# Attention and a gated feed-forward block on one core: DMA transposes replaced by TensorE transposes

## The chip, the cores and the metric

The kernel runs on one NeuronCore of a Trainium2 chip. The metric is the device time of one execution, in microseconds (us); lower is better. Before the change the median of three runs is 333.79 us.

## What is computed

Block-causal attention over 8 batches of 8 heads (576 positions, 64 columns a head) feeds a feed-forward block with a beta-swish. Inputs and the output are float32; inside, the matmuls take bf16 and fp16.

```python
# q, k, v: (8, 8, 576, 64)
scores = q @ k.T / sqrt(64)
mask   = (i // 64) >= (j // 64)              # a block sees itself and the blocks before it
attn   = softmax(where(mask, scores, -1e9))
x      = (attn @ v).transpose(0, 2, 1, 3).reshape(8 * 576, 512)
h      = x @ w_in                            # (4608, 2048)
out    = (h * sigmoid(beta * h)) @ w_out     # (4608, 512)
```

## The kernel before

The program is a list of operations that a planner in the file (class `Plan`, lines 49 to 347) orders before anything is emitted. Each operation has an engine, an assumed duration, dependencies, the buffers that it holds, and a priority. The planner simulates the five queues, the DMA rings and the eight PSUM banks with its own costs, and fixes one order for each engine; the engines then run their queues in order and wait on semaphores. A change of one operation therefore can move others.

The work has two halves that are woven together:

- **Attention**, in units `u = 4 * b + c`: batch b, pair of heads c. Q and K are loaded in float32 (line 749; lines 711 and 676 for the first two batches), cast to bf16 by GpSimd into `QKn` (lines 763, 767; 718), and turned so that the head's columns lie on the partitions, into `QKT`. In batches 0 and 1 TensorE turns them (line 727) and VectorE copies them out of PSUM (line 735). In the other six batches (`QB = 2`) one DMA transpose for two pairs of heads does it, on SyncE's queue (line 774): 22 blocks of 128 columns. Then come QK (line 818, and repeats by the helper at line 446; two heads at a time in half the array each), exp on ScalarE (line 839), attention times V with V's sums in a 65th column (line 882), and the reciprocal and the normalization on VectorE into `xq` (lines 894, 901).
- `xq` is turned too, into the ring `xT`, which holds 5 chunks of 512 rows. In batches 0 to 2 TensorE does it in 5 transposes a unit (line 930), and VectorE or ScalarE copies the 576 columns out (lines 940, 938), in two pieces or, at the end of the ring, three. From batch 3 on (`XB = 3`) a DMA transpose writes it from `xq` (line 918); it writes 640 columns, the last 64 of which the next batch overwrites.
- **Feed-forward**, in 9 chunks of 512 rows: 16 times the first matmul into one bank (line 1119), tanh on ScalarE (1129), and the gate on VectorE (1133) into `gT`; then the second matmul (line 1155 in chunk 0; in the others a form with seven products of half size, line 1040, with sums on VectorE at lines 984 and 1004 and results at 1061, 1064 and 1055), and the store.

The order around the change is set by priorities. Attention of batch b has the priority 994 + 100 * (b - 1.5) + 4.9 * c, chunk r of the feed-forward 1000 + 100 * r + j, so that attention runs about one and a half chunks ahead, and TensorE takes feed-forward matmuls while attention waits. Of the eight PSUM banks, pairs of banks (class "PP") serve QK and the products with V; single banks (class "P1") are banks 4 to 7 as long as pairs are still to come, and serve the first matmul, the second, and the turned pieces. Idle times of TensorE up to 50 us in the plan are filled by matmuls without use (line 534). SyncE's queue holds, in order, the loads of Q, K and V (lines 711, 749, 560, 563), the DMA transposes, and the last stores; ScalarE's queue issues the other stores (line 1071).

Of the kernel before, what the change touches and what calls it, by code (L numbers as in the profile page):

```python
# [16 lines left out]
RC = 512  # L17
# [342 lines left out]
def bass_blockwise_causal_attn__then__act_swish_beta_kernel(  # L360
# [10 lines left out]
    with es:  # L371
# [1 line left out]
            return es.enter_context(nc.sbuf_tensor(name, shape, dt))  # L373

        NQ = 2
        QB, XB, CAST = 2, 3, "POOL"
        NE = 3
        PARTS = [((0, 4, "SP", (4, 5, 0, 1, 2, 3)), (4, 8, "SP", range(2)), (4, 8, "POOL", (4, 5, 2, 3)))] + [((0, 8, "SP", range(6)),)] * 7
        GROUPS = [((0,), (1,), (2,), (3,))] + [((0, 1), (2, 3))] * 7
# [57 lines left out]
        def dve_t(n):  # L437
            return (n + 125) / 0.96
# [164 lines left out]
            return z  # L603


        def blocks(b):
            x0 = S * b % RX
            n = min(5, (RX - x0) // 128)
            return [z for z in ((0, n, x0), (n, 5 - n, 0)) if z[1]]

        xt = []
        early6 = []
        TC = "POOL"
# [2 lines left out]
        for u in range(NU):  # L616
# [126 lines left out]
            elif p == 0:  # L743

                for w, (nm, src) in enumerate((("Q", q), ("K", k))):
                    ts = P.tile("S4")

                    def fl(g, e, ts=ts, src=src, b=b, c=c, n=2 - w):
                        return [g.dma_start(STh[ts.slot].rearrange("p (i t) d -> p i (t d)", t=n),
                                            src[b, 2 * c:2 * c + 4].rearrange("h t d -> (h t d)").rearrange(  # L750
                                                "(i p x) -> p i x", p=128, x=64 * n))]

                    o = P.op("SP", QKI, fl, deps=[o for t in early6 for o in t.users] if b == QB else [],
                             tiles=[ts], xfer=(QX, QKX)[w], prio=u, dma=["d_S4", 0, 1])
                    o.two = w < 1
                    for i in range(2):
                        ld[nm, u + i] = o
                    for a in range(2):
                        def fn(g, e, ts=ts, tn=tn, a=a, w=w):
                            if w:  # L760
                                x = STh[ts.slot][:, 9 * a:9 * a + 5, :]
                                x = bass.AP(x.tensor, x.offset, [x.ap[0], [64, 5], [256, 2], [1, 64]])
                                return g.tensor_copy(QKn[tn.slot][:, a, 768:1408].rearrange("p (t h d) -> p t h d", t=5, h=2), x)  # L763
                            for i in range(2):
                                x = STh[ts.slot][:, 8 * a + i, :]
                                x = bass.AP(x.tensor, x.offset, [x.ap[0], [128, 3], [256, 2], [1, 64]])
                                z = g.tensor_copy(QKn[tn.slot][:, a, 384 * i:384 * i + 384].rearrange(  # L767
                                    "p (t h d) -> p t h d", t=3, h=2), x)
                            return z

                        casts.append(P.op(CAST, 740 if w else 1000, fn, deps=[o], tiles=[ts, tn], prio=u))

                def ft(g, e, tn=tn, td=tt_):
                    return [g.dma_start_transpose(QKT[td.slot][:].rearrange("c a (t n) -> c (a t) n", n=128),
                                                  QKn[tn.slot][:].rearrange("p a n -> p (a n)"))]

                turned = [P.op("SP", 3500, ft, deps=casts, tiles=[tt_, tn], xfer=3762, prio=-1, dma=["d_T", 0, 1])]
            tqk, cps = tt_, turned
            more = [tail] if b < QB else []
            ex = []  # L780
# [132 lines left out]
                m = P.op("DVE", dve_t(640), fm, deps=[av, r], tiles=[pv, ti, tx], prio=-6 if b < 1 else 0)  # L913
                m.same = [r]
            nrm = [m]
            if b >= XB:
                def fy(g, e, tx=tx, c=c, b=b):
                    return [g.dma_start_transpose(
                        xT[:, c, x0:x0 + 128 * n].rearrange("c (t n) -> c t n", n=128),
                        xq[xq_(tx)][:, t0:t0 + n, :].rearrange("p t n -> p (t n)")) for t0, n, x0 in blocks(b)]  # L920

                n = len(blocks(b))
                xt.append(P.op("SP", 1000 * n, fy, deps=nrm + (xt[u - 4:u - 3] if b > XB else []), tiles=[tx], xfer=855,
                               prio=-1, dma=[f"d_TX{n}_", 0, n]))
                continue
            px = P.tile("P1")

            def fx(g, e, tx=tx, px=px):
# [6 lines left out]
            def fy(g, e, px=px, c=c, b=b):  # L935
# [3 lines left out]
                    else:  # L939
                        z = g.tensor_copy(xT[:, c, x0:x0 + n], PSb[:, px.slot, t0:t0 + n])  # L940
                return z
            xt.append(P.op("ACT" if u in (2, 3) else "DVE", 600 if u in (2, 3) else 520, fy, deps=[xp], tiles=[px], prio=-6 if u < 4 else 0))

        for o in P.ops:
            if o.idx > 40 and o.engs == ("PE",) and not o.fill and any(d.engs == ("SP",) or d.engs == ("POOL",) for d in o.deps) and not o.rest:
# [162 lines left out]
        for r in range(NRC):  # L1108
            row = RC * r
            b0, b1 = row // S, (row + RC - 1) // S  # L1110
            xd = [xt[4 * b + c] for b in range(b0, b1 + 1) for c in range(4)]
            tg = P.tile("gT")
            gs, hs = [], []
            for j in range(NJ):
                ph, tt = P.tile("P1"), P.tile("th")

                def fh(g, e, ph=ph, j=j, row=row):
                    for c in range(4):
                        z = g.matmul(PS[:, ph.slot, :], w_in[:, c, 128 * j:128 * j + 128], xT[:, c, row % RX:row % RX + RC],  # L1119
                                     start=(c == 0), stop=(c == 3))  # L1120
                    return z

                o = P.op("PE", 4 * mm(512), fh, deps=xd + [win[j // 4]], tiles=[ph, tg], lat=4 * mm(512) + 170,
                         mode="full", prio=1000 + 100 * r + j)

                hs.append(o)

                def fs(g, e, ph=ph, tt=tt, j=j):
                    return g.activation(th[tt.slot][:], PS[:, ph.slot, :], ACT.Tanh, scale=beta[:, j:j + 1])  # L1129
                a = P.op("ACT", act_t(512, 1), fs, deps=[o, bC], tiles=[ph, tt], lat=act_t(512, 1) + 93, prio=0)  # L1130

                def fg(g, e, ph=ph, tt=tt, tg=tg, j=j):
                    return g.scalar_tensor_tensor(out=gT[tg.slot][:, j, :], in0=th[tt.slot][:], scalar=1.0,  # L1133
                                                  in1=PS[:, ph.slot, :], op0=ALU.add, op1=ALU.mult)
                gs.append(P.op("DVE", dve_t(512), fg, deps=[a] + (spare.users + spare_x.users if r == 1 else []), tiles=[ph, tt, tg], prio=0))

            for b in range(B):
                if any((S * b + a) // RC - RX // RC == r for a in (0, S - 1 if b < XB else 639)):
                    for c in range(4):
                        xt[4 * b + c].deps += hs  # L1140

            if r in FAST:
                fast(r, row, tg, gs)
                continue

            for w, d0, d1 in [(w, 0, DM) for w in range(4)]:
                po, to = P.tile("P1"), P.tile("ost")


                parts = [(4 * a, 4 * a + 4) for a in range(4)]  # L1150
                o = None
                for j0, j1 in parts:
                    def fo(g, e, po=po, tg=tg, w=w, j0=j0, j1=j1, d0=d0, d1=d1):
                        for j in range(j0, j1):
                            z = g.matmul(PS[:, po.slot, 0:d1 - d0], gT[tg.slot][:, j, 128 * w:128 * w + 128],  # L1155
                                         w_out[:, j, d0:d1], start=(j == 0), stop=(j == NJ - 1))
                        return z

                    n = (j1 - j0) * mm(d1 - d0)
                    was = o  # L1160
                    o = P.op("PE", n, fo, deps=gs[j0:j1] + wout[j0 // 4:(j1 + 3) // 4],
                             tiles=[po, tg], lat=n + 170, mode="full",
                             prio=1000 + 100 * r + (16 + w + 0.01 * j0 if w == 0 else
                                                     103 + 5.33 * (w - 1) + 1.33 * j0 / 4))
                    o.after = was
                    plain.append(o)

                def fv2(g, e, po=po, to=to, n=d1 - d0):
                    if e == "ACT":
                        return g.activation(ost[to.slot][:, 0:n], PS[:, po.slot, 0:n], ACT.Copy, scale=0.5)  # L1170
                    return g.tensor_scalar(out=ost[to.slot][:, 0:n], in0=PS[:, po.slot, 0:n], scalar1=0.5,
                                           scalar2=None, op0=ALU.mult)
                x = P.op("ACT", act_t(d1 - d0) + 80, fv2, deps=[o], tiles=[po, to], lat=act_t(d1 - d0) + 160, prio=0)

                def fd(g, e, to=to, row=row, w=w, d0=d0, d1=d1):
                    return [g.dma_start(out[row + 128 * w:row + 128 * w + 128, d0:d1], ost[to.slot][:, 0:d1 - d0])]
                P.op("ACT", 500, fd, deps=[x], tiles=[to], xfer=900, dma=["d_ost", to], prio=-1)
# [71 lines left out]
```

## Time and profile before

| | |
|---|---|
| three runs | 329.07, 333.79, 334.52 us |
| the profiled execution | 332.46 us, of which the span is 330.6 us |
| matmuls, TensorE's clock | 3062 records, 1.00 of full |
| DMA transposes | 12 from QKn to QKT, 24 from xq to xT |
| from issue to landing, median | 7.2 us and 2.7 us |
| DMA moved | 54.20 MB |
| SyncE's queue, share of 16 DMA engines | 61.9% |

A row of busy times gives the time in which an engine ran at least one instruction. Matmuls overlap: one lasts longer than the gap to the next. A row of the groups has the line, the engine, the operation, what is written from what, the number of instructions, the busy time and the mean of one in ns. A row of waits has who waited for whom, the total in us, how many times, and the longest. A chain of waits goes back from the last instruction to whatever released each step; a step on the chain isn't always time that the engine lost, as it may have had other work meanwhile. "PE" is TensorE, "PEld" its weight loads, "DVE" VectorE, "ACT" ScalarE, "POOL" GpSimd, "SPq" SyncE's queue.

### The profile page before, as it was taken

What the parts mean: (1) busy time and instruction counts of PE and PEld (TensorE: products, weight loads), DVE (VectorE), ACT (ScalarE), POOL (GpSimd) and SP (SyncE); (2) the same over time, 40 slices, a digit from 0 to 9 for tenths busy, and PEclk for the clock granted to TensorE, in tenths of its full rate; (3) what the DMA queues carried; (4) which work ended last, traced back from release to release, by engine and by line L of the source; (5) the groups of instructions that cost most, each with busy time, mean ns of one, the idle gap of its engine ahead of it and who ended that gap; (6) DMA issues with size and microseconds to landing.
All of it is one profiled execution on the core that took longest, in us unless ns stands there. A gap on an engine that the chain in (4) does not pass through costs nothing.

```text
span 330.6 us, 7365 instructions
## 1 busy us (share of the span) xinstructions
PE 317.3 (96%) x3062; PEld 197.5 (60%) x2979; DVE 220.3 (67%) x454; ACT 211.8 (64%) x316; POOL 91.5 (28%) x155
## 2 busy tenths in 40 slices
PE   7898999999999999999989999899999999999996
PEld 1363464435677557845655577655566766666685
DVE  5765883777754897367967684289576866666742
ACT  3857964396737976687678855676978445554521
POOL 5962290084183066003910650080000000000000
PEclk9999999999999999999999999999999999999999
DMA  7999999999899999959899999895030310111023
GB/s 221 251 227 238 205 241 197 204 260 234 187 300 215 207 229 217 234 112 217 173 180 184 235 264 205 202 209 110 0 73 2 103 34 32 33 64 35 3 92 129
DMA packets 147442, 54.20 MB, mean 164 GB/s; under 512 B 116672, under 2 KB 146896, under 8 KB 147408
## 3 DMA queue, kind: packets, MB, share of 16 engines
q1 hardware_dynamic: 132560, 40.72, 61.9%
q0 software_dynamic: 5568, 4.36, 8.4%
q10 hardware_dynamic: 9280, 8.65, 7.9%
q8 instruction: 24, 0.39, 0.5%
q14 instruction: 10, 0.08, 0.1%
HBM read 36.71 MB, written 9.44 MB: 140 GB/s over the span
## 4 chain that ended last, share of the span: by engine, by line
PE 64%; DMA 11%; SPq 8%; DVE 6%; POOL 4%; ACT 3%; issue 2%; POOLq 0%; ACTq 0%
PE PS L1119 25%; PE PS L1040 25%; SPq L560 5%; PE PS L818 5%; DMA ST<-in_q_dram 5%; PE PS L882 5%; DMA w_out<-in_moe_w_out_dram 4%; DVE gT L1133 2%; PE PS L1155 2%; ACT E L839 2%; POOL QKn L767 1%; DMA xT<-xq 1%; DVE xq L901 1%; DMA OV<-in_v_dram 1%; POOL Vn L587 1%
## 5 line engine op out<-in xcount | busy, mean ns | idle before, releaser
L1119 PE MATMUL PS<-xT,w_in 128*128 128x512 bf16 x540 | 129.9, 379 | 3.9 <-POOL QKn L763 1.1
L1129 ACT ACTIVATE th<-PS,beta 128x512 f32<-128x512 f32 x144 | 96.6, 701 | 54.4 <-PE PS L1119 49.8
L1133 DVE SCALAR_TENSOR_TENSOR gT<-th,PS 128x512 f16<-128x512 f32 x144 | 95.5, 681 | 34.9 <-ACT th L1129 34.1
L839 ACT ACTIVATE E<-PS 128x1024 bf16<-128x1024 f32 x93 | 92.1, 1031 | 14.6 <-PE PS L818 12.0
L1119 PEld LDWEIGHTS PS<-xT,w_in 128*128 128x128 bf16 x576 | 53.3, 98 | 56.9 <-DVE gT L1133 2.0
L1040 PE MATMUL PS<-w_out,gT 128*128 128x256 f16 x512 | 62.7, 273 | 0.0
L1040 PEld LDWEIGHTS PS<-w_out,gT 128*128 128x128 f16 x512 | 49.3, 98 | 11.0 <-issue 0.4
L587 POOL CAST Vn<-Vs 128x640 bf16<-128x640 f32 (+1 forms) x28 | 20.6, 734 | 101.8 <-DMA Vs<-in_v_dram 100.5
L1061 ACT ACTIVATE ost<-PS 128x512 f32<-128x512 f32 x32 | 19.2, 600 | 30.3 <-PE PS L1040 30.3
L882 PEld LDWEIGHTS PS<-Vn,E 128*128 128x128 bf16 x930 | 31.3, 97 | 5.7 <-DVE E L845 1.8
L882 PE MATMUL PS<-Vn,E 128*128 128x65 bf16 x930 | 32.5, 193 | 1.5 <-DMA xT<-xq 1.5
L818 PE MATMUL PS<-QKT 64*64 64x64 bf16 (+4 forms) x328 | 33.9, 295 | 0.0
L1040 PE MATMUL PS<-OV 128*128 128x256 f16 x256 | 32.3, 273 | 0.0
L767 POOL CAST QKn<-ST 128x384 bf16<-128x384 f32 x48 | 27.2, 594 | 5.5 <-DMA ST<-in_q_dram 2.8
L818 PEld LDWEIGHTS PS<-QKT 64*128 64x128 bf16 (+1 forms) x328 | 13.2, 96 | 25.4 <-issue 10.4
L1040 PEld LDWEIGHTS PS<-OV 128*128 128x128 f16 x256 | 24.0, 98 | 6.9 <-issue 1.9
L901 DVE TENSOR_TENSOR xq<-PS,inv 128x640 bf16<-128x640 f32 x31 | 25.3, 820 | 0.5
L1004 DVE TENSOR_TENSOR OV<-gT 128x1024 f16<-128x1024 f16 x32 | 22.6, 711 | 1.0 <-PE PS L1040 0.4
L845 DVE MEMSET E<- 64x64 uint32 x62 | 6.9, 112 | 22.0 <-ACT E L839 20.0
L1064 DVE SCALAR_TENSOR_TENSOR ost<-PS,ost 128x512 f32<-128x512 f32 x22 | 15.2, 689 | 9.0 <-PE PS L1040 4.5
L763 POOL CAST QKn<-ST 128x640 bf16<-128x640 f32 x24 | 18.8, 784 | 4.9 <-DMA ST<-in_k_dram 3.3
L1155 PE MATMUL PS<-w_out,gT 128*128 128x512 f16 x64 | 16.0, 380 | 0.5 <-DMA w_out<-in_moe_w_out_dram 0.5
(77 smaller groups left out, 185.0 us busy)
## 6 DMA issues: line engine op xcount, KB each, us to landing
out_dram<-ost ACTq DMA_DIRECT2D x32, 256.0 KB, 3.7
ST<-in_q_dram SPq DMA_DIRECT2D x12, 576.0 KB, 6.2
ST<-in_k_dram SPq DMA_DIRECT2D x12, 576.0 KB, 7.2
Vs<-in_v_dram SPq DMA_DIRECT2D x24, 256.0 KB, 4.3
ST<-in_q_dram SPq DMA_DIRECT2D x8, 256.0 KB, 6.2
ST<-in_k_dram SPq DMA_DIRECT2D x8, 256.0 KB, 6.5
w_in<-in_moe_w_in_dram POOLq DMA_DIRECT2D x4, 512.0 KB, 11.3
w_out<-in_moe_w_out_dram POOLq DMA_DIRECT2D x4, 512.0 KB, 10.6
```

Of the source, the lines that this page charges most:

```text
L587: return g.tensor_copy(Vn[t.slot][:, 0:n, g0:g1, 0:64], Vs[ts.slot][:, 0:n, g0:g1, :])
L767: z = g.tensor_copy(QKn[tn.slot][:, a, 384 * i:384 * i + 384].rearrange("p (t h d) -> p t h d", t=3, h=2), x)
L818: z = g.matmul(o, QKT[tqk.slot][r, uu % 2, 768 + 128 * t + y:768 + 128 * t + m + y], x)
L839: return g.activation(y, x, ACT.Exp, scale=0.125)
L882: z = g.matmul(o, eblk(te, t, i, h), Vn[Tv.slot][:, t, 2 * c + h, 0:65], start=(t == 0), stop=(t == i))
L901: return g.tensor_tensor(xq[xq_(tx)][:].rearrange("p i (h d) -> p h i d", h=2), both(pv, 0, 64), x, ALU.mult)
L1004: return P.op("DVE", dve_t(SZ * HC / 2), mk(lambda g: g.tensor_tensor(fo(), fx(), fy(), op)), deps=deps, tiles=tiles, prio=prio)
L1040: x = g.matmul(PS[:, pw.slot, HM * w:HM * w + HM], fa()[:, j, 128 * w:128 * w + 128], fb()[:, j, :], start=first and (pair or w == 0) and ...
L1119: z = g.matmul(PS[:, ph.slot, :], w_in[:, c, 128 * j:128 * j + 128], xT[:, c, row % RX:row % RX + RC], start=(c == 0), stop=(c == 3))
L1129: return g.activation(th[tt.slot][:], PS[:, ph.slot, :], ACT.Tanh, scale=beta[:, j:j + 1])
L1133: return g.scalar_tensor_tensor(out=gT[tg.slot][:, j, :], in0=th[tt.slot][:], scalar=1.0, in1=PS[:, ph.slot, :], op0=ALU.add, op1=ALU.mult)
L1155: z = g.matmul(PS[:, po.slot, 0:d1 - d0], gT[tg.slot][:, j, 128 * w:128 * w + 128], w_out[:, j, d0:d1], start=(j == 0), stop=(j == NJ - 1))
```

## The change

The two kinds of DMA transposes are taken out. For batches 2 to 7, each two pairs of heads of Q and K are turned by TensorE in 22 transposes, which go to three PSUM banks (8, 8 and 6 blocks); the first and the third are copied to `QKT` by VectorE, the second by ScalarE. The three bank operations depend on the same casts as the DMA transpose did, and have TensorE's priority of that unit. For batches 3 to 7, `xq` is turned as in the batches before: 5 transposes a unit into one bank, copied to `xT` in pieces. These copies go to ScalarE for units 2 and 3 as before, and now also for odd units from 5 on, otherwise to VectorE; the planner's assumed time for such a copy on VectorE is 700 instead of 520 ns from batch 2 on. The ring's rule for rows that are still in use loses its exception for the 640 columns.

```diff
-        QB, XB, CAST = 2, 3, "POOL"
+        QB, CAST = 2, "POOL"
+        TURN = ((0, 8, "DVE"), (8, 16, "ACT"), (16, 22, "DVE"))
...
-                def ft(g, e, tn=tn, td=tt_):
-                    return [g.dma_start_transpose(QKT[td.slot][:].rearrange("c a (t n) -> c (a t) n", n=128),
-                                                  QKn[tn.slot][:].rearrange("p a n -> p (a n)"))]
-
-                turned = [P.op("SP", 3500, ft, deps=casts, tiles=[tt_, tn], xfer=3762, prio=-1, dma=["d_T", 0, 1])]
+                turned = []
+                for n0, n1, eng in TURN:
+                    pt = P.tile("P1")
+
+                    def ft(g, e, tn=tn, pt=pt, n0=n0, n1=n1):
+                        x = QKn[tn.slot][:].rearrange("p a n -> p (a n)")
+                        for i in range(n0, n1):
+                            z = g.transpose(PSb[:, pt.slot, 128 * (i - n0):128 * (i - n0) + 128],
+                                            x[:, 128 * i:128 * i + 128], identB[:])
+                        return z
+
+                    n = n1 - n0
+                    o = P.op("PE", n * 56, ft, deps=casts, tiles=[tn, pt, tt_], lat=n * 56 + 170, mode="full", prio=pr(u))
+
+                    def fc(g, e, td=tt_, pt=pt, n0=n0, n1=n1):
+                        y = QKT[td.slot][:].rearrange("c a n -> c (a n)")[:, 128 * n0:128 * n1]
+                        x = PSb[:, pt.slot, 0:128 * (n1 - n0)]
+                        return g.activation(y, x, ACT.Copy) if e == "ACT" else g.tensor_copy(y, x)
+
+                    turned.append(P.op(eng, act_t(128 * n) if eng == "ACT" else dve_t(128 * n), fc, deps=[o],
+                                       tiles=[pt, tt_], prio=0))
...
-            if b >= XB:
-                def fy(g, e, tx=tx, c=c, b=b):
-                    return [g.dma_start_transpose(
-                        xT[:, c, x0:x0 + 128 * n].rearrange("c (t n) -> c t n", n=128),
-                        xq[xq_(tx)][:, t0:t0 + n, :].rearrange("p t n -> p (t n)")) for t0, n, x0 in blocks(b)]
-
-                n = len(blocks(b))
-                xt.append(P.op("SP", 1000 * n, fy, deps=nrm + (xt[u - 4:u - 3] if b > XB else []), tiles=[tx], xfer=855,
-                               prio=-1, dma=[f"d_TX{n}_", 0, n]))
-                continue
...
-            xt.append(P.op("ACT" if u in (2, 3) else "DVE", 600 if u in (2, 3) else 520, fy, deps=[xp], tiles=[px], prio=-6 if u < 4 else 0))
+            on = "ACT" if u in (2, 3) or u > 4 and u % 2 else "DVE"
+            xt.append(P.op(on, 600 if on == "ACT" else 700 if b > 1 else 520, fy, deps=[xp], tiles=[px], prio=-6 if u < 4 else 0))
...
-                if any((S * b + a) // RC - RX // RC == r for a in (0, S - 1 if b < XB else 639)):
+                if any((S * b + a) // RC - RX // RC == r for a in (0, S - 1)):
```

More of the change, by code (lines that the diff above doesn't have):

```diff
@@ L603, in pieces @@
             return z
[L606 to L609, printed above, removed]
         xt = []
```

## The prediction

> **What bounds the kernel now.** I read the page first: busy shares, then the costliest groups, then PE's busy time by stretch, then what PE waited for, and only then the chain of waits.
>
> ```profile
> span 330.6 us, 7365 instructions
> PE 317.3 (96%) x3062; PEld 197.5 (60%) x2979; DVE 220.3 (67%) x454; ACT 211.8 (64%) x316; POOL 91.5 (28%) x155
> ```
>
> PE is busy for 96% of the span, and the engines that empty PSUM for two thirds of it. Is a busy PE also a full one? The skill page "Perfetto Trace Analysis" (Identifying the Most-Contended Engine) says that matmul occupancy is a poor measure of this and that weight-load occupancy is a better one. That speaks against me: weight loads are busy for only 60%, so by this rule there could be room for more PE work. The chain of waits in order of time has a stretch that settles it:
>
> ```profile
> 313.03 0.86 PE PS L1119 x4
> 313.89 13.99 PE PS L1040 x128
> ```
>
> 128 matmuls of line 1040 in 13.99 us are 109 ns apart, and four of line 1119 in 0.86 us are 215 ns apart. Their columns (256 and 512) scale as these gaps do: the stream is packed at one rate. The room is therefore the idle time. By stretch (columns: stretch, its length, then busy time of PE, PEld, DVE, ACT, POOL):
>
> ```profile
> 0.00:60.00 60.00, 54.86 (x625) 27.32 (x559) 38.32 (x100) 37.33 (x56) 30.54 (x65) 1.00 1.13 226
> 60.00:260.00 200.00, 194.97 (x1955) 122.34 (x1930) 139.15 (x287) 143.35 (x213) 60.91 (x90) 1.00 0.90 182
> 260.00:331.00 71.00, 67.50 (x486) 47.81 (x491) 42.87 (x68) 31.12 (x47) 0.00 (x0) 1.00 0.18 59
> ```
>
> Of 13.3 us of idle time 5.1 lie before 60 us, in the start that the change hardly touches, and 3.5 after 260 us, where only the feed-forward part runs. In between, where the change acts, PE is idle for 200 - 194.97 = 5.0 us. That is all that anything can fill or recover there. What these waits are, PE alone, from 60 to 260 us:
>
> ```profile
> PE PS L882 <- DMA xT<-xq: 1.5, 1, 1.5
> PE PS L1119 <- POOL QKn L763: 1.1, 1, 1.1
> PE PS L930 <- DVE xq L901: 0.6, 1, 0.6
> ```
>
> One wait of 1.5 us is for a DMA transpose. The second, put down to POOL, stands before a matmul that doesn't read QKn; the weight load of the same group is released by VectorE's line 1004, so I don't count it as the transposes' doing. Thus the DMA transposes cost PE 1.5 us.
>
> **Removed.** 12 DMA transposes of QKn (line 774) and 24 of xq (line 918) on SP's queue, with their issue times (median 4.4 us and 1.3 us), their DMA traffic, and SP's waits ahead of them, which hold back the loads queued behind. Worth at PE: the 1.5 us. Loads will start earlier, but what is late for want of them is POOL's casts, and behind these the same QK matmuls; PE has feed-forward matmuls to do meanwhile, and that cover is why so little shows. The drop of the 640th column from the ring rule (639 becomes S-1) frees ring space earlier; no wait on it is seen, so I count nothing; if it had hidden a wait, that lies within the 5.0.
>
> **Added to PE.** For batches 2 to 7, two pairs of heads at a time, 22 transposes: 12 x 22 = 264. For batches 3 to 7, 20 units of 5: 100. Together 364. The price, from the same operations before (lines 727 and 930), in the timeline of PE:
>
> ```profile
> 32.78 0.39 PE L727 MATMUL PS<-identB,QKn 128*128 128x128 bf16 x4
> 33.01 1.03 PE L1119 MATMUL PS<-xT,w_in 128*128 128x512 bf16 x4
> ```
>
> Four transposes begin at 32.78 and the next matmul at 33.01: 0.23 us, 57 ns each; in the trace's single starts the median gap is 56 ns. The 219 ns that each lasts is latency, overlapped by the next. 364 x 56 ns = 20.4 us. Here a rule stands far off: "TensorE: Matmul & The Clock Gate" (Part 4: PE-mode transpose) gives 390 ns alone and some 275 ns inside a kernel, and says that transposes don't count as activity for the clock. By it the sum would be 364 x 275 = 100 us, a time of 434 us. The row decides for 56: these transposes stand between matmuls, and the granted clock reads 9 in all 40 slices, those with transposes too. For a lower end nothing is to be had below 56, as no transposes overlapped.
>
> Where do the 20.4 us lie? Each lands in a packed stream, 60 to 260 us, so on the path, except for what falls into the 5.0 us of idle. They don't need further changes of tiling mode: they are full-array work beside other full-array work.
>
> **New waits on PE.** PE runs in order. A bank of QK transposes waits for POOL's casts (as the QK matmuls did, by way of the DMA), an x unit for VectorE's normalization (line 901). Behind a waiting transpose stand all later matmuls, and behind those ScalarE's tanh and exp. The nearest row: in 60 to 260 us the four x units of batch 2 cost 0.6 us of PE idle, 0.15 each. For 20 units: 3.0 us. Bounds: 0, if the planner's order always leaves room, and for all 56 pieces, QK banks too, the rate of all twelve old units, start included: ahead of them PE and its weight loads sat idle for 1.5 (until xq), 0.9 and 0.6 us (until QKT and gT), 3.0 us or 0.25 each, which makes 14 us. I take 3.0.
>
> **Added to VectorE and ScalarE.** VectorE's dense copies out of PSUM: 409 ns for 512 columns, 181 for 64 (line 940), so 0.51 ns a column, 0.67 us for 1024 and 0.54 for 768. (Line 735 takes 686 ns for 512, but reads with a stride; the new copy doesn't. At that rate a bank of 1024 would be about 1.4 us.) ScalarE: 597 and 218 ns (line 938), so 1.03 us for 1024. Per group of two pairs DVE 1.21 us, ACT 1.03 us, twelve times 14.5 and 12.4. Units of x, 0.59 us on DVE, 0.82 on ACT: DVE gains 10 and gives up 4 (units 5, 7, 9, 11 move), +3.5 us; ACT gains 14, +11.4 us. In the middle stretch ACT goes from 143 of 200 us to some 166 of 220, DVE from 139 to 158 (about 172 at the strided rate): 75% and 72%. Neither becomes the bound, so PE's work covers them; without that cover they would cost up to 24 us on ACT. What is queued behind a copy on ScalarE is the next tanh or exp, and behind that a PSUM bank: part of the 14 us bound.
>
> **PSUM.** 36 banks and 20 x banks are taken for some 1.4 us each (0.45 filling, 0.2 latency, 0.7 emptying), 80 bank-us over 220 us x 4 banks = 9%. No row prices this; its cost is inside the bounds of the new waits (0 to 14 us); more tenants can't make a bank free sooner, so it is no gain.
>
> **Sum.** Against the profiled execution (332.46 us, of which 330.6 are span): 332.5 + 20.4 - 1.5 + 3.0 = 354.4. Against the median of the runs, 333.79, the same +21.9: **355.7 us**.
>
> **Rivals.**
> (a) All idle of the middle stretch is recovered, because loads are early and x comes without a queue, and nothing waits anew: 333.8 + 20.4 - 5.0 = 349.2. For it: PE has other work at nearly all times. Against: most of the 5.0 us are short waits for ScalarE and VectorE, which get more to do.
> (b) In-order waits and full banks: 333.8 + 20.4 - 1.5 + 14 = 366.7. For it: the 0.25 us before the old x units, and 75% of ScalarE. Against: in the old middle stretch the units cost 0.15, and the planner knows of every new operation.
> (c) Not slower: the DMA path was the pace-setter. The chain of waits runs through it:
>
> ```profile
> 143.66 1.26 SPq L918
> ...
> 150.74 10.21 DMA ST<-in_q_dram
> ...
> 204.36 3.36 DMA xT<-xq
> ```
>
> A transpose's issue, held on SP, delays the loads behind it. SP's issues from 143.66 to 150.7 sum to 5.6 us, the load is 10.2 us, and the piece at 203.1 to 207.7 is 4.2 us: 20.0. If all that were time of the end, the result were 333.8 + 20.4 - 20.0 = 334.2, no change. It decides from 13.7 us on (20.4 less 2% of 333.8). Against it: between 60 and 260 us PE is idle for 5.0 us in all; while the chain ran through SP, PE did other work that had to be done anyway.
> (d) The skill's 275 ns: 434 us.
>
> **How the numbers follow.** Likeliest, 0.67: 355.7, own range 351 to 360. (a) 0.10, (b) 0.18, (c) 0.04, (d) 0.01. What a measurement can tell from no change is about 2%: 327.1 to 340.5. Only (c) lies there; 0.01 of its chance I give to a time below. So faster 0.01, same 0.03, slower 0.96. The range takes in (a), and (b) up to nearly its end: 348 to 365.
>
> **What would show it.** PE busy up by some 20 us at the same share (95 to 96%); starts of the new transposes 56 ns apart; PE's idle before the x transposes near 3 us, and gone for DMA xT; ACT near 236, DVE near 238 us busy; the SP queue without waits, loads landing earlier, with no gain at the end. I am wrong if PE's share falls below 93% (then b), if the gap is well over 56 ns (d), or if PE's busy time rises and the span doesn't (c).

## The result, and the profile after

The changed kernel takes 355.98 us (median of four runs, 354.81 to 357.46) against 332.2 us for the kernel before in the same runs: a ratio of 1.075, with a 95% interval of 1.064 to 1.086. It is slower, and the time forecast was 355.7. The profiled execution has a span of 353.8 us, 23.2 more than before. Three of the four executions of the changed kernel, the profiled one among them, had a mean granted clock of 0.995, and the one at 1.00 took 354.81 us.

The head of the page after, then TensorE's time by stretch (the middle stretch is 20 us longer now; columns as before), then what TensorE waited for:

```profile
span 353.8 us, 8098 instructions
PE 338.8 (96%) x3418; PEld 218.0 (62%) x3343; DVE 234.5 (66%) x492; ACT 232.9 (66%) x358; POOL 89.3 (25%) x155
```

```profile
0.00:60.00 60.00, 54.08 (x629) 27.36 (x564) 38.51 (x98) 38.90 (x59) 30.59 (x65) 0.97 1.09 222
60.00:280.00 220.00, 214.03 (x2266) 141.04 (x2249) 148.66 (x316) 159.53 (x247) 58.68 (x90) 1.00 0.50 115
280.00:354.00 74.00, 70.68 (x526) 49.60 (x531) 47.28 (x79) 34.47 (x53) 0.00 (x0) 1.00 0.14 50
```

```profile
PE PS L1122 <- DVE gT L1136: 2.1, 2, 1.6
PE PS L776 <- ACT QKT L786: 1.4, 2, 0.7
PE PS L1158 <- DMA w_out<-in_moe_w_out_dram: 1.4, 1, 1.4
PE PS L1122 <- ACT QKT L786: 1.3, 3, 0.5
```

TensorE is busy for 21.5 us more at the same share of 96%, and the span is 23.2 us longer. The load on the DMA engines in the middle fell from 0.90 to 0.50, and no gain at the end came of it. The wait for a DMA transpose of x is gone. In its place stand waits for ScalarE's copy out of a bank (line 786), ahead of the next transposes (line 776) and of feed-forward matmuls (line 1122, which was line 1119): 2.7 us together. That is too much by some 0.65 us. The page has 532 matmuls of line 1122 and all 576 of their weight loads, so 44 records are missing, and a matmul without a record counts as idle time. Each of the three waits at line 1122 stands where the first matmul of a group has no record (12 weight loads and 11 matmuls in the group from 139.77 us on), and 216 ns of each were work. The page of the kernel before lacks 36 records in the same way, so both shares of 96% are a little low. These are the groups of new work:

```profile
L776 PE MATMUL PS<-identB,QKn 128*128 128x128 bf16 x264 | 17.9, 219 | 1.4 <-ACT QKT L786 1.4
L932 PE MATMUL PS<-identB,xq 128*128 128x128 bf16 x155 | 13.9, 220 | 0.4 <-DVE QKT L731 0.4
L786 ACT ACTIVATE QKT<-PS 128x1024 bf16<-128x1024 bf16 x12 | 12.3, 1026 | 11.5 <-PE PS L776 11.5
L786 DVE COPY QKT<-PS 128x1024 bf16<-128x1024 bf16 x12 | 8.2, 686 | 1.9 <-PE PS L776 1.9
L786 DVE COPY QKT<-PS 128x768 bf16<-128x768 bf16 x12 | 6.6, 552 | 7.9 <-PE PS L776 7.7
```

The new transposes start 56 ns apart (median gap of single starts) and last 219 ns, as the old ones did. The copies cost 1.03, 0.69 and 0.55 us, where 1.03, 0.67 and 0.54 were reckoned. (Of the transposes of line 932, 60 are those of batches 0 to 2 and not new.)

### The profile page after: what moved, and what is told of

It is laid out like the page before. It is cut to its first block, busy times and chain, and to the rows that moved or that the text cites. A ratio compares the mean times of both kernels' runs of the same rounds, so it can differ in the third digit from the quotient of the medians.

```text
span 353.8 us, 8098 instructions
## 1 busy us (share of the span) xinstructions
PE 338.8 (96%) x3418; PEld 218.0 (62%) x3343; DVE 234.5 (66%) x492; ACT 232.9 (66%) x358; POOL 89.3 (25%) x155
## 4 chain that ended last, share of the span: by engine, by line
PE 85%; DMA 6%; ACT 4%; DVE 3%; issue 1%; POOL 1%; ACTq 0%; POOLq 0%
PE PS L1122 33%; PE PS L1043 28%; PE PS L830 7%; PE PS L894 6%; DMA w_out<-in_moe_w_out_dram 4%; PE PS L776 3%; PE PS L932 3%; PE PS L1158 2%; DMA ST<-in_k_dram 1%; DVE OV L987 1%; ACT QKT L786 1%; PE PS L447 1%; ACT E L851 1%; PE PS L723 1%; ACT th L1132 1%
## 5 line engine op out<-in xcount | busy, mean ns | idle before, releaser
L1043 PE MATMUL PS<-w_out,gT 128*128 128x256 f16 x512 | 63.6, 273 | 0.0
L588 POOL CAST Vn<-Vs 128x640 bf16<-128x640 f32 (+1 forms) x28 | 22.8, 813 | 83.7 <-PE PS L894 67.9
L763 POOL CAST QKn<-ST 128x384 bf16<-128x384 f32 x48 | 23.1, 511 | 25.2 <-PE PS L776 24.0
L1007 DVE TENSOR_TENSOR OV<-gT 128x1024 f16<-128x1024 f16 x32 | 21.7, 684 | 0.3
L786 DVE COPY QKT<-PS 128x1024 bf16<-128x1024 bf16 (+1 forms) x24 | 14.7, 619 | 9.8 <-PE PS L776 9.6
L786 ACT ACTIVATE QKT<-PS 128x1024 bf16<-128x1024 bf16 x12 | 12.3, 1026 | 11.5 <-PE PS L776 11.5
L776 PE MATMUL PS<-identB,QKn 128*128 128x128 bf16 x264 | 17.9, 219 | 1.4 <-ACT QKT L786 1.4
## 6 DMA issues: line engine op xcount, KB each, us to landing
w_out<-in_moe_w_out_dram POOLq DMA_DIRECT2D x4, 512.0 KB, 10.7
```

The source lines that it names most:

```text
L588: return g.tensor_copy(Vn[t.slot][:, 0:n, g0:g1, 0:64], Vs[ts.slot][:, 0:n, g0:g1, :])
L776: z = g.transpose(PSb[:, pt.slot, 128 * (i - n0):128 * (i - n0) + 128], x[:, 128 * i:128 * i + 128], identB[:])
L786: return g.activation(y, x, ACT.Copy) if e == "ACT" else g.tensor_copy(y, x)
L1043: x = g.matmul(PS[:, pw.slot, HM * w:HM * w + HM], fa()[:, j, 128 * w:128 * w + 128], fb()[:, j, :], start=first and (pair or w == 0) and ...
```

## The experiments

Two theories were on trial: that the change costs TensorE's own time, a transpose at 56 ns each, and that the copies and the waits behind them cost it; and the rival of the other side, that the DMA path had been the pace. Runs of one group shared the runs of the kernel before, whose median was 331.5 us in the first group of four, 332.0 in the second and 331.3 in the third.

### The two halves of the change

Only Q and K are turned by TensorE: the change without the lines of x.

```diff
+        QB, XB, CAST = 2, 3, "POOL"      # x: DMA transposes kept
+        TURN = ((0, 8, "DVE"), (8, 16, "ACT"), (16, 22, "DVE"))
```

> Only Q and K are turned by TensorE; x stays with the DMA transposes. Theory (price of PE's own time): 264 transposes x 56 ns = 14.8 us over the kernel before, whose median is 332.2 us: 347 us, PE busy near 332 us. The saved DMA traffic and issue times of the 12 large transposes give nothing visible. Rival (the DMA path was worth something and the x part spoils it): below 343. Rival (waits on new banks are a good part of the cost): above 351.

Measured: 348.79 us, 1.0495 times before (1.0419 to 1.0571). The medians differ by 17.3 us: 14.8 and 2.5 on top. TensorE's waits for ScalarE's copies out of the banks come to 2.1 us here.

Only x is turned by TensorE: the change with the DMA transpose of line 774 kept in place of the three banks.

```diff
-                for n0, n1, eng in TURN:
...
+                turned = [P.op("SP", 3500, ft, deps=casts, tiles=[tt_, tn], xfer=3762, prio=-1, dma=["d_T", 0, 1])]
```

> Only x is turned by TensorE; Q and K stay with the DMA transposes. Theory: 100 x 56 ns = 5.6 us, less the 1.5 us wait for a DMA transpose of x, plus 3.0 us of waits for the normalization: 332.2 + 7.1 = 339.3 us; with the Q and K part alone (+14.8) the two parts add up to the change's +22 or +23.8. Rival (each part adds waits that the other hides): the sum of the two parts is over 28 us. Rival (contention of both parts for PSUM and ScalarE is the cost): the sum is under 18 us.

Measured: 335.94 us, 1.0116 times before (1.0034 to 1.0198): 4.5 us more by the medians, 1.1 to 6.6 by the interval. The 5.6 us of the transposes alone lie in it; the 7.1 that were expected do not. The 3.0 us of new waits for the normalization did not come: TensorE waits for it once, for 0.6 us, as in the kernel before. The halves sum to 21.8 us, the whole cost 23.8: neither rival about their sum holds. TensorE in the middle stretch of this run:

```profile
60.00:260.00 200.00, 199.00 (x2039) 127.02 (x1990) 137.36 (x297) 147.80 (x238) 58.37 (x90) 1.00 0.79 168
```

It is idle for 1.0 us there. So a small part of the x transposes may have lain where TensorE had been idle.

### More and less work on TensorE

The same plan, each transpose of Q and K done twice:

```diff
-                        for i in range(n0, n1):
+                        for i in [*range(n0, n1)] * 2:
```

> The changed kernel with each transpose of Q and K done twice (the second writes the same bank again), in an unchanged plan, so that all queues but PE's are the same. Theory: 264 more transposes at 56 ns: 356.0 + 14.8 = 370.8 us. Rival (the cost of the change is latency, copies and waits, and PE has room): under 362. Rival (a transpose costs its full 219 ns when dense): over 400.

Measured: 366.67 us (366.19 to 367.07), 10.7 more than the changed kernel. The gaps of the 528 transposes are 56 ns in the median, so they were not cheaper; TensorE's share rose to 98%. By the medians 14.8 us of work cost 10.7.

The same plan, one matmul a bank in place of its transposes:

```diff
-                        for i in range(n0, n1):
-                            z = g.transpose(PSb[:, pt.slot, 128 * (i - n0):128 * (i - n0) + 128],
-                                            x[:, 128 * i:128 * i + 128], identB[:])
-                        return z
+                        m = 64 * (n1 - n0)
+                        return g.matmul(PS[:, pt.slot, 0:m], identB[:], x[:, 128 * n0:128 * n0 + m])
```

> The changed kernel with the 8, 8 and 6 transposes of each group of Q and K replaced by one matmul of 512, 512 and 384 columns that fills the same bank, so that Q and K are not turned (the attention is computed on other values); copies, waits and plan are unchanged. A group then takes PE 216 + 216 + 162 ns in place of 22 x 56 = 1232 ns: 12 x 0.64 = 7.7 us less. Theory: 356.0 - 7.7 = 348.3 us. Rival (copies out of the banks and waits for them set the time): within 2 us of 356.

Measured: 349.2 us (348.3 to 350.21), 6.8 less, of 7.7. The time follows TensorE's work in both directions, which the theory of copies alone can't give.

The two differences are not yet those of the edits. The eight executions of these two runs had a clock of 0.999 or 1.00, and most of those behind the 355.98 us did not. As the plan is the same, the traces can be laid side by side, instruction by instruction. In the changed kernel's, TensorE waits 1.0 us for a copy on ScalarE (line 645) from 6 us on, and then has half the clock for 3.4 us. The columns are as before, the clock third from the end:

```profile
5.00:10.00 5.00, 3.43 (x31) 1.22 (x23) 2.04 (x4) 1.88 (x5) 2.84 (x5) 0.77 1.10 313
```

From 15 us to the first transposes of the change, at 53 us, it is 1.2 us later than the two runs. Counted from there on, the doubling cost 11.9 us and one matmul for each bank saved 6.1. So 2.9 of the 14.8 us lay in time that TensorE had lost before: 1.7 in waits for ScalarE's copies, and 1.1 between 55 and 68 us in waits for the load of w_out and for a gate behind it.

### The copies out of the banks

The same plan, copies of 64 columns in batches 4 to 7:

```diff
-                    def fc(g, e, td=tt_, pt=pt, n0=n0, n1=n1):
+                    def fc(g, e, td=tt_, pt=pt, n0=n0, n1=n1, m=128 * (n1 - n0) if b < 4 else 64):
```

> The changed kernel, in an unchanged plan, with the copies out of the three banks of Q and K cut to 64 columns in batches 4 to 7, so that those batches attend with old values; TensorE does all its transposes. Gone are 8 x (0.69 + 0.55 - 0.36) = 7.0 us of VectorE and 8 x (1.03 - 0.23) = 6.4 us of ScalarE. Theory (TensorE's time is the cost): at most the waits for ScalarE's copies vanish, 1.4 + 1.3 = 2.7 us in the profile: 353.3 to 356 us. Rival (the copies are on the path): 356.0 - 6.4 = 349.6 us or less.

Measured: 351.22 us (351.09 to 351.87), 4.8 less. By the medians this lies between the two theories. Side by side, 1.7 of the 4.1 us between the two traces are there by 68 us, long before the first short copy: 1.2 from the start, the rest from the load of w_out and the gate behind it. The other 2.4 us arise at four places, the two groups of batches 4 and 6 and the matmuls behind them, all of which waited for ScalarE's copies. In batch 4 the two groups now follow without a pause:

```profile
133.70 2.77 PE L776 MATMUL PS<-identB,QKn 128*128 128x128 bf16 x44
```

So ScalarE's copies cost about 2.4 us here, and the shorter copies of VectorE gained nothing that can be seen.

All three banks copied by VectorE:

```diff
-        TURN = ((0, 8, "DVE"), (8, 16, "ACT"), (16, 22, "DVE"))
+        TURN = ((0, 8, "DVE"), (8, 16, "DVE"), (16, 22, "DVE"))
```

> The changed kernel with the middle bank of each group copied by VectorE as well (the planner makes a new order): ScalarE loses 12.3 us of busy time, VectorE gains 8.2 us. Theory: both are covered, and the 2.7 us of waits for ScalarE's copies turn into waits for VectorE or vanish: 353 to 357 us. Rival (ScalarE's load is what the change costs): 344 us. Rival (VectorE is near its limit): over 360 us.

Measured: 351.69 us (351.35 to 353.83), 4.3 less, slightly below the expected band. VectorE has more to do and the kernel is faster. The order is a new one, and the wait for the load of w_out is gone too, so the 4.3 us are not those of the copies alone. What TensorE waits for now, and its middle stretch:

```profile
PE PS L723 <- POOL QKn L714: 1.2, 2, 0.7
...
PE PS L1122 <- DVE gT L1136: 0.8, 2, 0.5
PE PS L776 <- ACT xT L940: 0.5, 1, 0.5
```

```profile
60.00:260.00 200.00, 198.68 (x2088) 129.03 (x2041) 146.95 (x308) 138.37 (x220) 58.81 (x90) 1.00 0.54 122
```

The waits of TensorE's matmuls for line 786 are no longer among them. Where they arose in the changed kernel can be read in the order of time; the two groups of batch 4 come one behind the other:

```profile
135.42 1.46 PE L776 MATMUL PS<-identB,QKn 128*128 128x128 bf16 x22
...
136.23 1.24 DVE L786 COPY QKT<-PS 128x1024 bf16<-128x1024 bf16 x2
136.51 1.02 ACT L786 ACTIVATE QKT<-PS 128x1024 bf16<-128x1024 bf16 x1 [0.84 <-PE PS L776]
...
137.59 1.40 PE L776 MATMUL PS<-identB,QKn 128*128 128x128 bf16 x22 [0.71 <-ACT QKT L786]
...
140.00 2.32 PE L1122 MATMUL PS<-xT,w_in 128*128 128x512 bf16 x10 [0.47 <-ACT QKT L786]
```

TensorE fills three banks in 1.2 us. The four banks of class P1 are then soon used up, and the second group begins only when ScalarE has emptied its bank, at 137.53: 0.71 us of idle. It is not ScalarE's load, which is 66%: its copy began at 136.51, as soon as its bank was full, and took 1.02 us. It is the time from a full bank to an empty one.

Then both together, in the plan of the last run. First the transposes doubled:

> Each transpose of Q and K twice, with all bank copies on VectorE, in the plan of the run with all copies on VectorE (351.7 us). Doubling alone cost 10.7 us in place of 14.8. Theory (the missing 4.1 us were PE's waits for ScalarE's copies, under which the second pass lay; without these waits the price is whole): 351.7 + 14.8 = 366.5 us, no shorter than the doubled run with ScalarE's copies (366.7). Rival (a repeated transpose is simply cheaper, some 40 ns): 351.7 + 10.7 = 362.4 us.

Measured: 365.58 us (365.31 to 366.25): 13.9 more, of 14.8. Without the waits for ScalarE's copies and for w_out the price is nearly whole. The rival of a cheaper repeat is out.

And one matmul for each bank:

> One matmul for each bank in place of its transposes (Q and K not turned), with all bank copies on VectorE, in the plan of the run with all copies on VectorE. Theory (TensorE's own time alone is left): 351.7 - 7.7 = 344.0 us. Rival (with less on TensorE the copies come to set the time): 347 us or more.

Measured: 350.0 us (348.43 to 350.62), only 1.7 less, of 7.7. Here the rival is right about the time, and the waits say how much of it is the copies:

```profile
PE PS L1158 <- DMA w_out<-in_moe_w_out_dram: 1.9, 2, 1.7
PE PS L776 <- DVE QKT L786: 1.8, 4, 0.7
```

```profile
PEld PS L776 <- DVE QKT L786: 4.3, 7, 1.1
```

Filling three banks now takes TensorE 0.6 us, emptying them takes VectorE 2 x 0.69 + 0.55 = 1.9 us. The matmuls wait for it 1.8 us, and 0.4 more at line 1122; the weight loads' 4.3 us are in part the same time and don't add to that. Another 1.9 us are a wait for the load of w_out, which the run with all the transposes didn't have, and 1.2 us are waits for other work of VectorE and ScalarE (lines 1007 and 1064). So the copies are part of the loss; TensorE, with less to do, also reaches other waits sooner. With transposes it takes TensorE 1.2 us to fill the banks, and the copies keep up better.

### The DMA path

The kernel before, in the same plan, with the DMA transposes of Q and K cut to one block in batches 4 to 7:

```diff
-                def ft(g, e, tn=tn, td=tt_):
+                def ft(g, e, tn=tn, td=tt_, a=22 if b < 4 else 1):
...
+                    ... QKT[td.slot][:].rearrange("c a (t n) -> c (a t) n", n=128)[:, 0:a],
+                        QKn[tn.slot][:].rearrange("p a n -> p (a n)")[:, 0:128 * a]
```

> The kernel before, in an unchanged plan, with the DMA transposes of Q and K of batches 4 to 7 cut from 22 blocks to one each, so that those batches attend with old values in most of QKT. 8 x 21 x 32 KB = 5.5 MB of DMA traffic and most of eight issue times are gone, and TensorE's work is as before. Theory (the DMA transposes hardly cost TensorE anything): 331.5 us less at most 1.5, so 330 to 331.5. Rival (the chain through SP and the DMA is the pace): two thirds of 20 us less, 318 us.

Measured: 330.6 us, 0.9963 times before (0.9941 to 0.9984): 1.2 us less. TensorE's wait of 1.5 us for a DMA transpose of x is gone. The chain through SP and the DMA was not the pace.

```profile
PE 319.4 (97%) x3098; PEld 197.4 (60%) x2979; DVE 220.9 (67%) x454; ACT 211.9 (64%) x316; POOL 90.5 (27%) x155
```

```profile
60.00:260.00 200.00, 197.83 (x1988) 123.43 (x1940) 141.06 (x289) 144.56 (x215) 59.91 (x90) 1.00 0.73 156
```

This run also corrects a reading. TensorE runs the same matmuls in the same order as in the kernel before, yet the page has 3098 of them and the page of before 3062: 36 records of line 1119 are missing there. Set against their weight loads, which are all there, 24 of those lie in the middle stretch. With a matmul put in for each, the 5.0 us of idle in the prediction shrink to some 3.2 us, an estimate; the rest was work.

One step in the other direction, x of batches 1 and 2 by DMA as well:

```diff
-        QB, XB, CAST = 2, 3, "POOL"
+        QB, XB, CAST = 2, 1, "POOL"
```

> The kernel before with one step in the other direction: x of batches 1 and 2, too, goes by DMA transposes, 40 transposes fewer on TensorE. Theory: 331.5 - 40 x 56 ns = 329.3 us. Rival (at that time the DMA queues are full, so x comes late and TensorE waits): over 333 us.

Measured: 343.91 us (339.13 to 345.75), 1.029 times before (1.021 to 1.037), and 12 us more instead of 2 less. From 60 us on:

```profile
60.00:90.00 30.00, 24.94 (x195) 11.85 (x190) 18.03 (x35) 17.15 (x25) 9.93 (x16) 0.89 1.06 214
90.00:120.00 30.00, 23.91 (x296) 17.59 (x284) 13.91 (x33) 16.34 (x23) 9.68 (x16) 0.92 1.15 229
```

TensorE is idle for 5.1 and 6.1 us and gets a lower clock; the DMA engines are full. One wait there, of 2.8 us, is for the DMA transpose of QKT. The cause is not settled by this: the DMA engines were as full in these stretches of the kernel before (1.08 and 1.10), the planner made a new order, and the other waits are for exp, the masking behind it and the normalization. What is shown is that the small price of the DMA path doesn't carry over to two batches more. That made two hybrids worth a run. Q and K of batch 2 alone by TensorE:

```diff
+                if b == 2:
+                    turned = []
+                    for n0, n1, eng in TURN:         # all three "DVE"
...
+                else:
                     def ft(g, e, tn=tn, td=tt_):
```

> The kernel before, with Q and K of batch 2 alone turned by TensorE and copied by VectorE: that is where the first DMA transpose takes 11.4 us on SP and the DMA engines are full. 44 transposes x 56 ns = 2.5 us. Theory (PE's time is the price wherever it is paid): 332 + 2.5 = 334.5 us. Rival (early DMA relief is worth more than that): under 331 us, and faster than both kernels.

Measured: 334.79 us, 1.0082 times before (1.0057 to 1.0108): 2.7 us more by the ratio, 3.5 by the medians; about the price of 44 transposes, and no relief. And x of batch 3 by TensorE:

```diff
-        QB, XB, CAST = 2, 3, "POOL"
+        QB, XB, CAST = 2, 4, "POOL"
```

> The kernel before, with x of batch 3 turned by TensorE too: 20 transposes x 56 ns = 1.1 us more, four DMA transposes fewer in the stretch from 109 to 140 us, where the DMA engines are full. Theory: 333.1 us. Rival (as one batch more on the DMA cost 12 us for two batches, one batch less gains): under 330 us.

Measured: 331.08 us, 0.9986 times before (0.9966 to 1.0005): neither the 1.1 us more nor a gain that can be told from none. No version run here was clearly faster than the kernel before, apart from the one that left work out.

## Why the prediction was right, point by point

**TensorE sets the time: right.** The stream was packed, and what was added to it was paid. Twice the transposes, and about half of their work, moved the time with it; 13.9 of 14.8 us once the waits for ScalarE's copies were out of the way. Less work is another matter: with all copies on VectorE the same saving of 7.7 us gave 1.7. The Trainium skill, "Perfetto Trace Analysis" (Identifying the Most-Contended Engine), judges TensorE's headroom by the weight-load share, together with the matmuls' throughput. At 60% that share looks like room; 14.8 us of further work on a kernel with 62% still cost 11.9.

**56 ns for a transpose, 20.4 us: right.** The 275 ns of rival (d) would have made 100 us. The granted clock read 1.00 from 60 us on, also in the run with 528 of them. In the first stretch of the changed kernel's profiled execution it read 0.97; the half clock there ended at 11 us, and the first transposes of the change came at 53.

**The DMA transposes removed, 1.5 us: about right.** Two thirds of those of Q and K were worth 1.2 us. The 20 us of the rival (c) were on the chain, but not on TensorE. What the trace couldn't tell is that the small price doesn't carry over: two batches more on the DMA cost 12 us.

**New waits, 3.0 us for x: about right in size, wrong in place.** The step said that the x transposes would wait for the normalization at 0.15 us each. They did not: x alone cost 4.5 us, and the only wait of TensorE ahead of line 932 in the changed kernel is one of 0.4 us, for a copy of QKT. Instead some 2.5 us came at the banks of Q and K, by ScalarE's copies: 2.5 on top of the transposes in the run with Q and K alone, and 2.4 where the trace with the short copies parts from the changed kernel's. The prediction had them only within its upper bound, as part of (b). Its sentence that TensorE's work covers the copies holds for their load and not for their delay: each group takes three of four banks at once, and in batches 4 and 6 two groups follow one another. The bound itself was too wide: it added the waits of matmuls and of their weight loads, which overlap. The matmuls alone waited 1.0 us ahead of the twelve old units, and at that rate 56 pieces make 4.7 us and not 14.

**5.0 us that could be recovered: too much.** 24 matmuls in that stretch had no record, and some 3.2 us are left. (The 3.5 us given for the stretch after 260 us are 3.1, as the span ends at 330.6; the sum of 13.3 has that right.)

**The base, 333.79 us: high.** It was the median of three runs. The kernel before had medians of 332.2, 331.5, 332.0 and 331.3 us in the groups of the result and of the experiments. The rise forecast was 21.9 us, the rise measured 23.8.

That the time came out within 0.3 us is luck, twice over. Two terms erred against each other: x was forecast at 5.6 - 1.5 + 3.0 = 7.1 us and cost 4.5, Q and K at 14.8 and cost 17.3. Their sum, 21.8 us, is the 21.9 forecast. And the whole rose by 2.0 us more than the halves, about as much as the base was too high (1.6). Of these 2.0 us the profiled execution shows 1.2 in its first 15 us, before anything of the change runs; the rest stays open and is within the noise of such differences. No run parts the planner's new order from the work that it orders. ScalarE and VectorE were busy for 232.9 and 234.5 us, a little less than the 236 and 238 forecast.

## What to carry to other kernels

Where one engine's stream is packed, price moved work by the gap between starts of the same instruction in that stream, not by its duration, and take what it replaces as free unless the packed engine waited for it; a long stretch of other queues on the chain of waits is no saving by itself. Work that lands in PSUM brings a second bill: count how many banks it wants at once and how long one takes from full to empty, since an engine at 66% can still be late. Before idle time is called room, compare the number of records with the number of instructions in the program. And before a small difference of medians is put down to an edit, lay the two traces side by side: here over a third of one lay ahead of anything that the edit touched.

## What the runs showed of the hardware

A dense copy of 1024 bf16 columns out of PSUM took VectorE 686 ns, just what the old copy of 512 columns with a strided read took (line 735, 686 ns). A dense copy of 512 columns took 409 ns (line 940), so the strided one took 1.7 times as long.

In the run with more DMA transposes TensorE was busy for only 1.65 of the 5 us from 65 us on, and had a clock of 0.56 in the next 5:

```profile
65.00:70.00 5.00, 1.65 (x11) 0.49 (x7) 1.29 (x2) 1.06 (x2) 0.00 (x0) 1.00 1.15 237
70.00:75.00 5.00, 3.47 (x18) 1.51 (x19) 0.40 (x4) 3.62 (x7) 2.19 (x4) 0.56 1.21 277
75.00:80.00 5.00, 5.00 (x50) 2.17 (x47) 2.25 (x7) 3.79 (x6) 4.56 (x9) 0.76 1.28 247
```

From 72.74 us on eight matmuls of line 1119 take 3.60 us, where 216 ns from one to the next would make 1.9:

```profile
72.74 3.60 PE L1119 MATMUL PS<-xT,w_in 128*128 128x512 bf16 x8
```

The same follows the idle time from 110 us on: 1.69 of 5 us busy, then a clock of 0.50 in the next 5. In the changed kernel's trace the half clock near 8 us also follows a wait. In these three places lost time was thus followed by slow matmuls; that the one brings the other is not shown by any run here. It is part of the 12 us.
